# Attention and a feed-forward net in one kernel: another order of TensorE's work in the attention lead, the split of the attention's output on ScalarE and VectorE, and the closing flag placed earlier in the program

## The chip, the cores and the metric

The kernel runs on one core of a Trainium2 chip. It uses TensorE (PE, with its weight loads listed as PEld), VectorE (DVE), ScalarE (ACT), GpSimd (POOL) and SyncE (SP, which issues the DMAs). The metric is the device time of one execution in microseconds (us). The profile is one execution with the hardware profiler on; its span goes from the first to the last recorded instruction.

## The reference

```python
def _attn_ref(q, k, v, n_global, n_local):            # (4, 8, 768, 64) each; n_global 8, n_local 96
    scores = q @ k.transpose(0, 1, 3, 2) / sqrt(64)
    pos = arange(768); rel = pos[:, None] - pos[None, :]
    is_global = pos[None, :] < n_global
    is_local = (rel >= 0) & (rel < n_local)
    dist = where(is_global & ~is_local, n_local, abs(rel))
    scores = scores - slopes[:, None, None] * dist    # slope of head h: 2 ** -(h + 1)
    scores = where(is_global | is_local, scores, -1e9)
    a = exp(scores - max(scores)); a = a / (sum(a) + 1e-9)
    return a @ v

def _moe_ref(x, w_in, w_out):                         # x (3072, 512), w_in (512, 2048), w_out (2048, 512), float64
    h = x @ w_in
    return maximum(0.01 * h, h) @ w_out               # returned as float32
```

The attention's output, put together over the heads, is x of the second function. The weights come as 64-bit floats.

## The kernel before

**Work.** The 3072 tokens are 24 *steps* of 128. Six steps make one sequence, and a step that is not its sequence's first has block index `i > 0`. Each step is two *units* of four heads, so there are 48 units, u = 0 to 47. For its 128 queries a unit looks only at the keys that the band can reach: per half of the queries a `near` set of 128 keys (32 global, 96 earlier) and 64 of its `own`, which makes `KW` = 192 columns per head. The attention runs in plain float32. The feed-forward net (FFN) takes *chunks* of three steps, 384 tokens, and 16 blocks of 128 hidden features; a number j counts the blocks in the order in which they are done (7 of chunk 0, then 16 of chunk 1, the rest of chunk 0, then chunks 2 to 7). Each of its products is three TensorE matmuls in a rounded 32-bit format: every factor is split into a high part (the rounded value) and a low part (the rest), and high times high, high times low and low times high are summed. So the attention's output becomes `xh` and `xl`, the hidden layer `gh` and `gl`, the weights `wih`/`wil` and `woh`/`wol`.

**A unit's path.** `scores(u)`: 8 matmuls (L176) into a PSUM tile, `ps_sc` in the lead and `ps_av` later. `biased(u)`: four DVE instructions (L190) that add the band's table and take the maximum. `exps(u)`: four ACT exponentials (L205) that also give the sums. `sums(u)`: two small DVE instructions (L225, L226) for the reciprocals, then for units under 14 POOL makes `dg` (L240), diagonal matrices of the reciprocals. `transposes(u)`: 24 matmuls (L263) of probabilities by `dg`, which transpose and normalize into `ps_tr`. `keep_pt(u)`: one ACT copy to SBUF, `pt` (L278). `attn_v(u)`: probabilities times values, 4 matmuls (L302) for the own part and 16 (L309) for the near part. `keep_x(u)`: an ACT copy (L316) of the result to `x`; `split_x(u)`: POOL rounds `x` to `xh` (L44) and subtracts for `xl` (L329). Units from 14 on are transposed by DVE and DMAs in place of `transposes` and `keep_pt`.

**Events.** `event(t)` works on three units at once: scores of t, transposes of t-1 and attn_v of t-2. Events 0 to 7 are the *lead*, ahead of the first FFN block; events 8 to 13 are run with FFN blocks j = 1 to 6. From event 22 on two units are handled together (`visit`). In the lead the PE order within an event is scores, transposes, attn_v; from event 8 on it is attn_v, scores, transposes. The lead's PSUM tiles lie in a pool `ps_lead` that is closed before those of the FFN (`ps_h`, `ps_o`) are opened, so the first FFN matmul waits until the last `ps_ov` has been read.

**Weights.** 32 pieces of 64-bit weights are loaded and rebuilt as 32-bit values (`split_float64`): scale (ACT, L524), shift (DVE, L527 and L529), low (DVE, L533), then one event or FFN block later the high part (ACT, L537) and the rest (DVE, L540). Pieces 0 to 6 are converted in the lead, and the table `conv_at` gives piece 7 to j = 0, 8 to j = 1, 9 to j = 2, 10 and 11 to j = 3, and so on.

**What sets the order.** Engines run their own queues in program order. Nearly all instructions here are pinned to the order in which the code is written; the others (the FFN's copies in quiet blocks, DMAs of the output, the flag) are placed by a scheduler.

**FFN block.** `hidden` does 12 matmuls (L753 to L755) into `ps_h`, an ACT copy to `t` (L757), a DVE leaky ReLU (L758), the ACT cast to `gh` (L763) and the DVE difference `gl` (L764). `project` adds 3 matmuls per step (L774 to L776) into one of three `ps_o` tiles. The FFN for block j is followed on PE by the projections of block j-1. At a chunk's end the sums are copied to `part` (L440 by DVE, L442 by ACT) and SP sends them out (L444).

**The end.** `band_holds` checks, from the data's counts and maxima, whether the band is wide enough, and makes one integer flag. Every engine loads it into a register (L791), and where it is 0 the general path (`general_attention`, `general_ffn`) would compute all of it again. With these inputs it is not run, but every engine jumps over its instructions (the branch of L793) before the closing barrier (L848).

## Time and profile before

| | |
|---|---|
| time, median of 3 runs (lowest to highest) | 657.39 us (657.39 to 660.11) |
| the profiled execution's own time | 656.46 us |
| its span | 654.7 us, 14749 instructions |
| first FFN matmul starts | 40.15 us |
| first FFN matmul of j = 1, 2, 3, 4 | 46.43, 54.4, 60.9, 67.5 us |
| last FFN matmul ends | about 648 us |
| last DMA of the output issued | 648.63 us |

A line of a timeline reads: start, duration, engine, line of the kernel, operation, output <- inputs, tile and shape, count; in brackets the engine's idle time before it and what released it. A line of windows gives the length of the stretch, then busy time and instruction count of PE, PEld, DVE, ACT and POOL, the share of TensorE's full clock that was granted, the DMA share and GB/s. A line of waits gives the total, the number and the longest.

### The profile page before, as it was taken

Reading aid. Unit: us, or ns where it says so; the run is one execution under the profiler, and the core shown is the slowest. Engines: PE = TensorE matmul, PEld = TensorE weight load, DVE = VectorE, ACT = ScalarE, POOL = GpSimd, SP = SyncE. Lnnn points to the kernel's source line nnn. Section 1 sums busy time; section 2 is a strip of 40 time slices with the busy share of each in tenths; the row PEclk is TensorE's granted clock in tenths of the full one; section 3 lists DMA queues with packets and bytes.
Section 4 is the critical chain, followed back from the end, with each engine's and each line's share of the span. In section 5 each row is a group of like instructions: output and inputs, shape, how many; then the busy total and the mean of one; then the engine's idle time right before and its main releaser. Section 6 shows DMA issues by size and latency. Waiting matters only on the chain.

```text
span 654.7 us, 14749 instructions
## 1 busy us (share of the span) xinstructions
PE 628.5 (96%) x5803; PEld 558.1 (85%) x5803; DVE 363.6 (56%) x1073; ACT 281.3 (43%) x796; POOL 82.0 (13%) x146
## 2 busy tenths in 40 slices
PE   5689999999999999999999999999999999999995
PEld 4577888988888888988989889889889889999994
DVE  6949978987566444545645535535545546232221
ACT  6848765455444342442442433434433424232221
POOL 3424620000111010110110110100110101100000
PEclk9869999999999999999999999999999999999999
DMA  8966554432666433343444444335343432010001
GB/s 286 358 216 199 192 157 140 145 97 89 209 218 217 145 91 113 130 162 115 162 130 139 137 129 133 126 108 170 118 147 129 155 116 88 12 49 2 1 0 54
DMA packets 55166, 88.09 MB, mean 135 GB/s; under 512 B 9776, under 2 KB 30256, under 8 KB 55088
## 3 DMA queue, kind: packets, MB, share of 16 engines
q1 hardware_dynamic: 55088, 87.06, 40.6%
q8 instruction: 48, 0.79, 0.5%
q14 instruction: 30, 0.25, 0.1%
HBM read 67.90 MB, written 19.14 MB: 133 GB/s over the span
## 4 chain that ended last, share of the span: by engine, by line
PE 85%; DVE 6%; ACT 4%; POOL 2%; issue 2%; DMA 0%; ACTq 0%; DVEq 0%; POOLq 0%
PE ps_h L753 13%; PE ps_h L754 13%; PE ps_o L776 13%; PE ps_h L755 13%; PE ps_o L774 12%; PE ps_o L775 12%; PE ps_v L176 3%; PE ps_v L309 2%; ACT pr L205 1%; PE ps_v L302 1%; DVE w L533 1%; DVE w L529 1%; ACT w L524 1%; PE ps_av L176 1%; DVE t L758 1%
## 5 line engine op out<-in xcount | busy, mean ns | idle before, releaser
L753 PE MATMUL ps_h<-xh,wih 128*128 128x384 f32 x512 | 175.9, 343 | 1.2 <-ACT x L316 1.2
L754 PE MATMUL ps_h<-xl,wih 128*128 128x384 f32 x512 | 172.7, 337 | 0.7 <-POOL xl L329 0.7
L755 PE MATMUL ps_h<-xh,wil 128*128 128x384 f32 x512 | 172.4, 337 | 0.0
L758 DVE SCALAR_TENSOR_TENSOR t<-t 128x384 f32<-128x384 f32 x128 | 72.3, 565 | 150.6 <-ACT t L757 150.4
L776 PE MATMUL ps_o<-woh,gl 128*128 128x512 f32 x384 | 151.8, 395 | 0.1
L774 PE MATMUL ps_o<-woh,gh 128*128 128x512 f32 x384 | 150.4, 392 | 1.1 <-ACT part L442 0.7
L775 PE MATMUL ps_o<-wol,gh 128*128 128x512 f32 x384 | 150.5, 392 | 0.0
L757 ACT COPY t<-ps_h 128x384 f32<-128x384 f32 x128 | 61.1, 477 | 186.1 <-PE ps_h L755 186.1
L753 PEld LDWEIGHTS ps_h<-xh,wih 128*128 128x128 f32 x512 | 96.6, 189 | 11.5 <-ACT x L316 4.5
L764 DVE TENSOR_TENSOR gl<-t,gh 128x384 fp32r<-128x384 f32 x128 | 74.5, 582 | 55.6 <-ACT gh L763 55.6
L754 PEld LDWEIGHTS ps_h<-xl,wih 128*128 128x128 f32 x512 | 96.7, 189 | 5.2 <-POOL xl L329 0.9
L763 ACT CAST gh<-t 128x384 fp32r<-128x384 f32 x128 | 65.6, 512 | 74.2 <-DVE t L758 73.3
L755 PEld LDWEIGHTS ps_h<-xh,wil 128*128 128x128 f32 x512 | 96.6, 189 | 0.0
L776 PEld LDWEIGHTS ps_o<-woh,gl 128*128 128x128 f32 x384 | 72.1, 188 | 17.3 <-DVE gl L764 1.9
L205 ACT ACTIVATE pr<-pr,nmall 128x192 f32<-128x192 f32 (+1 forms) x192 | 83.6, 439 | 3.6 <-DVE nmall L190 3.5
L774 PEld LDWEIGHTS ps_o<-woh,gh 128*128 128x128 f32 x384 | 72.0, 188 | 12.9 <-ACT part L442 1.2
L775 PEld LDWEIGHTS ps_o<-wol,gh 128*128 128x128 f32 x384 | 72.1, 188 | 11.1
L44 POOL TENSOR_SCALAR xh<-x 128x256 fp32r<-128x256 f32 x48 | 21.3, 445 | 435.2 <-ACT x L316 366.3
L190 DVE CUSTOM_DVE_ANT_0 pr<-ps_v,nbw 128x192 f32<-128x192 f32 x88 | 26.2, 354 | 32.6 <-ACT x L316 32.6
L329 POOL TENSOR_TENSOR xl<-x,xh 128x256 fp32r<-128x256 f32 x48 | 37.3, 778 | 4.0
L205 ACT ACTIVATION_READ_ACCUMULATOR pr<-pr,nmall 128x1 f32 x192 | 36.6, 191 | 0.0
L232 DVE TENSOR_SCALAR pr<-pr,rs 128x192 f32<-128x192 f32 (+1 forms) x136 | 33.7, 312 | 1.0
(93 smaller groups left out, 495.0 us busy)
## 6 DMA issues: line engine op xcount, KB each, us to landing
kr<-in_kp_dram SPq DMA_DIRECT2D x40, 384.0 KB, 4.0
vr<-in_vp_dram SPq DMA_DIRECT2D x40, 320.0 KB, 4.4
via<-pr SPq DMA_DIRECT2D x30, 384.0 KB, 2.6
pt<-via SPq DMA_DIRECT2D x120, 96.0 KB, 2.3
wst<-in_wi_dram SPq DMA_DIRECT2D x16, 512.0 KB, 4.6
wst<-in_wo_dram SPq DMA_DIRECT2D x16, 512.0 KB, 3.7
qs<-in_qp_dram SPq DMA_DIRECT2D x24, 256.0 KB, 3.7
out_dram<-part SPq DMA_DIRECT2D x21, 256.0 KB, 2.4
```

What stands on the lines that cost most here:

```text
L205: pin(nc.scalar.activation(out=p, in_=p, func=AF.Exp, scale=-1.0, bias=nm[:, 2 * a + j:2 * a + j + 1], accum_out=sm[:, 2 * a + j:2 * a + j ...
L329: pin(nc.gpsimd.tensor_tensor(out=xl, in0=x, in1=xh.bitcast(F32), op=ALU.subtract))
L753: tc.keep_in_program_order(nc.tensor.matmul(ps, lhsT=wih[:, k, fs], rhs=xh[:, k, :CT], start=(k == 0), stop=False))
L754: tc.keep_in_program_order(nc.tensor.matmul(ps, lhsT=wih[:, k, fs], rhs=xl[:, k, :CT], start=False, stop=False))
L755: tc.keep_in_program_order(nc.tensor.matmul(ps, lhsT=wil[:, k, fs], rhs=xh[:, k, :CT], start=False, stop=(k == NK - 1)))
L757: pin(nc.scalar.copy(out=t, in_=ps))
L758: pin(nc.vector.scalar_tensor_tensor(out=t, in0=t, scalar=0.01, in1=t, op0=ALU.mult, op1=ALU.max))
L763: pin(nc.scalar.copy(out=gh, in_=t))
L764: pin(nc.vector.tensor_tensor(out=gl, in0=t, in1=gh.bitcast(F32), op=ALU.subtract))
L774: tc.keep_in_program_order(nc.tensor.matmul(o, lhsT=gh[:, ts_], rhs=woh[:, f, :], start=first, stop=False))
L775: tc.keep_in_program_order(nc.tensor.matmul(o, lhsT=gh[:, ts_], rhs=wol[:, f, :], start=False, stop=False))
L776: tc.keep_in_program_order(nc.tensor.matmul(o, lhsT=gl[:, ts_], rhs=woh[:, f, :], start=False, stop=last))
```

## The change

It has six parts.

1. **PE order in the lead.** `event` does scores(t), attn_v(t-2), transposes(t-1); transposes and attn_v have changed places.
2. **`tall` units** (2 to 11: transposed by PE and not first in their sequence). The near keys of a query half now lie across all 128 partitions of `pt`: per head and half one matmul of 64 rows by 128 columns makes them (8, new line 265), and the own keys keep 8 of 64 by 64 (new line 275), 16 in place of 24. The near part of `attn_v` takes 8 matmuls over 128 rows in place of 16 over 64 (new line 327). The values are laid out to match on the host.
3. **The split of x.** `high_x` is an ACT copy from PSUM that rounds right into `xh`; `low_x` (new line 344) is a DVE subtraction of `xh` from PSUM. POOL's two instructions and the tile `x` are gone. In event 7 `high_x(5)` stands ahead of the exponentials; `low_x` stands behind them from event 7 on, and at the event's end before. In `visit`, `low_x` follows both `biased`.
4. **Conversions.** Piece 7 is converted between the lead and the first FFN block; the blocks j = 0 to 6 take pieces 8 to 14, one each.
5. **The flag.** `band_holds` (without its transpose and identity) is written four FFN blocks before the end, a 1 by 1 matmul that sums over the partitions three blocks before the end, and the load of the flag ahead of the last chunk's copies.
6. **The general path.** Its loop over the heads, unrolled before, is now two loops that run, its DMAs go to GpSimd's queue in place of SP's, and its copies to DVE in place of ACT.

```diff
+    def tall(u):
+        return u < BY_DVE and where(u)[2] > 0
...
+        if tall(u):
+            for n in range(4):
+                for f in range(2):
+                    rows = slice(f * HALF, (f + 1) * HALF)
+                    tc.keep_in_program_order(nc.tensor.matmul(ps[:, f, n * HALF:(n + 1) * HALF],
+                                     lhsT=pr[rows, n * KW:n * KW + 2 * HALF], rhs=dg[rows, n % 2 * 2 + n // 2, :],
+                                     start=True, stop=True))
         for j in range(2):
-            for g in range(0 if i else 1, 3):
+            for g in range(2 if tall(u) else 1, 3):
...
         for f in range(0 if i else 1, 2):
-            for g in range(0 if i else 1, 2):
+            for g in (0,) if tall(u) else range(0 if i else 1, 2):
                 for j in range(2):
                     for a in range(2):
+                        if tall(u):
+                            n = 2 * j + a
+                            lhs, rhs = v[:, n, f, :], pt[:, n, f]
+                        else:
+                            lhs, rhs = v[rows, 2 * f + g, j, :], near(rows, j, g, f)
...
-    def keep_x(u, av):
-        x = att.tile([P, 2, P], F32, name="x", bufs=1)
-        pin(nc.scalar.copy(out=x, in_=av[:, :, 2 * KW:]))
-    def split_x(u):
-        pin(copy_exact(nc.gpsimd, xh, x))
-        pin(nc.gpsimd.tensor_tensor(out=xl, in0=x, in1=xh.bitcast(F32), op=ALU.subtract))
+    def high_x(u, av):
+        pin(nc.scalar.copy(out=parts(u, 0), in_=av[:, :, 2 * KW:]))
+    def low_x(u, av):
+        units.pop(u)
+        pin(nc.vector.tensor_tensor(out=parts(u, 1), in0=av[:, :, 2 * KW:], in1=parts(u, 0).bitcast(F32), op=ALU.subtract))
...
             scores(t, av)
-            if mid:
-                transposes(t - 1)
             if old:
                 ov = ps_lead.tile([P, 2, 512], F32, tag="ps_ov", name="ps_ov")
                 attn_v(t - 2, ov)
+            if mid:
+                transposes(t - 1)
...
             biased(t, av)
+            if t == LEAD + 1:
+                high_x(t - 2, ov)
             exps(t)
+        if t > LEAD:
+            low_x(t - 2, ov)
...
-        if old and t < LEAD + 2:
-            keep_x(t - 2, ov)
-        if old:
-            split_x(t - 2)
+        if old and t <= LEAD:
+            high_x(t - 2, ov)
+        if old and t <= LEAD:
+            low_x(t - 2, ov)
...
+        if c == NCHUNK - 1:
+            flags.append(nc.values_load(flag, min_val=0, max_val=1, ...))
...
-    conv_at = {0: [7], 1: [8], 2: [9], 3: [10, 11], 4: [12], 5: [13], 6: [14]}
+    conv_at = {n: [n + LEAD_CONV + 1] for n in range(half)}
...
+    for step in (*due, *conversion(LEAD_CONV)):
+        if step in due:
+            due.remove(step)
+        step()
...
+        if j == len(order) - NF // 4:
+            fl = const.tile([P, 4], F32, name="fl")
+            band_holds(tc, fl, nvec, nmall)
+        if j == len(order) - NF // 4 + 1:
+            band_holds_everywhere(tc, fl, ps_x.tile([P, 2, 512], F32, tag="ps_t", name="ps_f")[0:1, 0, 0:1], flag)
...
-            for h in range(H):
...
-                nc.sync.dma_start(out=q_sb, in_=qt[bass.ds(b, 1), h].rearrange("o d s -> (o d) s"))
...
+            with tc.For_i(0, H // 2, 1) as hp:
+                with tc.For_i(0, 2, 1) as two:
...
+                    nc.gpsimd.dma_start(out=q_sb, in_=qt[bass.ds(b, 1), bass.ds(hp, 1), bass.ds(two, 1)].rearrange("o g h d s -> (o g h d) s"))
...
```

Three places show what the edits do to the engines' own order. The first is PE at the lead's last event, 7, up to the first FFN matmul (`ps_sc` are scores, `ps_tr` transposes, `ps_ov` the attention's outputs). Before:

```order
L176 MATMUL ps_sc<-kr,qs 64x192 x8
L263 MATMUL ps_tr<-dg,pr 64x64 x24
L302 MATMUL ps_ov<-pt,vr 64x128 x4
L309 MATMUL ps_ov<-pt,vr 64x64 x16
L753 MATMUL ps_h<-xh,wih 128x384
```

and after:

```order
L180 MATMUL ps_sc<-kr,qs 64x192 x8
L315 MATMUL ps_ov<-pt,vr 64x128 x4
L327 MATMUL ps_ov<-pt,vr 64x64 x8
L265 MATMUL ps_tr<-dg,pr 128x64 x8
L275 MATMUL ps_tr<-dg,pr 64x64 x8
L797 MATMUL ps_h<-xh,wih 128x384
```

Scores stand first in both; the outputs have moved ahead of the transposes, and both have fewer, larger matmuls.

The second place is DVE from the last lead event's conversion work to the first FFN block (`w` with a number is the piece being rebuilt, `rs` the reciprocals of event 7, `t` and `gl` the FFN's first block). Before:

```order
L540 TENSOR_TENSOR wol<-w_650,woh 128x512
L527 TENSOR_SCALAR w_739<-w_739 128x512
L529 SCALAR_TENSOR_TENSOR w_739<-wst,w_739 128x512
L225 TENSOR_SCALAR rs<-sm 128x4
L226 RECIPROCAL rs<-rs 128x4
L533 SCALAR_TENSOR_TENSOR w_739<-wst,w_739 128x512
L758 SCALAR_TENSOR_TENSOR t<-t 128x384
L540 TENSOR_TENSOR wil<-w_739,wih 128x4x128
L764 TENSOR_TENSOR gl<-t,gh 128x384
L527 TENSOR_SCALAR w_799<-w_799 128x512
```

and after:

```order
L344 TENSOR_TENSOR xl<-ps_ov,xh 128x2x128
L576 TENSOR_TENSOR wol<-w_587,woh 128x512
L563 TENSOR_SCALAR w_658<-w_658 128x512
L565 SCALAR_TENSOR_TENSOR w_658<-wst,w_658 128x512
L229 TENSOR_SCALAR rs<-sm 128x4
L230 RECIPROCAL rs<-rs 128x4
L569 SCALAR_TENSOR_TENSOR w_658<-wst,w_658 128x512
L576 TENSOR_TENSOR wil<-w_658,wih 128x4x128
L563 TENSOR_SCALAR w_694<-w_694 128x512
L565 SCALAR_TENSOR_TENSOR w_694<-wst,w_694 128x512
L569 SCALAR_TENSOR_TENSOR w_694<-wst,w_694 128x512
L802 SCALAR_TENSOR_TENSOR t<-t 128x384
```

The low part of x is now DVE's, and the end of piece 6 with the whole of piece 7 stands ahead of the first FFN block's `t`.

The third place is SP at the program's end. Before:

```order
L444 DMA out_dram<-part 128x512 x6
L791 TENSOR_LOAD flag
L793 COMPARE_AND_BRANCH
L672 COMPARE_AND_BRANCH
L672 UNCONDITIONAL_BRANCH x2
L848 BRANCH_PREFETCH_HINT
L672 ISA
L677 DMA gq<-in_qt_dram 64x768
```

and after:

```order
L469 DMA out_dram<-part 128x512 x6
L448 TENSOR_LOAD flag
L835 COMPARE_AND_BRANCH
L710 COMPARE_AND_BRANCH
L710 UNCONDITIONAL_BRANCH x2
L894 BRANCH_PREFETCH_HINT
```

The flag's load still stands behind the last output DMAs on SP, and on ACT and DVE behind the last copies. What lies behind the branch is shorter: from the flag's load to the end SP has 26 rows in place of 162, ACT 27 in place of 240, DVE 215 in place of 527 and PE 332 in place of 446, while POOL has 76 in place of 29.

## The prediction

> **What bounds the kernel now.** I read the page first, its engines and its chain of waits.

> ```profile
> span 654.7 us, 14749 instructions
> ...
> PE 628.5 (96%) x5803; PEld 558.1 (85%) x5803; DVE 363.6 (56%) x1073; ACT 281.3 (43%) x796; POOL 82.0 (13%) x146
> ...
> PE 85%; DVE 6%; ACT 4%; POOL 2%; issue 2%; DMA 0%; ACTq 0%; DVEq 0%; POOLq 0%
> ```

> TensorE (PE) is busy 96% of the span and carries 85% of the chain, so only its holes and its own work can change the time. The windows say where the holes are (columns: busy time and count of PE, PEld, DVE, ACT, POOL, then the granted clock).

> ```profile
> 20.20:30.40 10.20, 5.60 (x245) 4.36 (x240) 10.06 (x38) 9.51 (x28) 5.82 (x9) 1.00 0.99 350
> 30.40:44.10 13.70, 10.65 (x175) 9.50 (x174) 6.31 (x20) 6.55 (x22) 4.31 (x7) 0.50 0.81 284
> 46.40:86.30 39.90, 37.54 (x645) 33.24 (x637) 38.23 (x104) 30.56 (x89) 21.49 (x34) 1.00 0.64 207
> ...
> 500.00:600.00 100.00, 100.00 (x770) 90.04 (x769) 40.66 (x116) 33.39 (x87) 7.36 (x14) 1.00 0.24 79
> ```

> In the lead, 20 to 30 us, DVE is full (10.06 of 10.20) and ACT nearly so, PE half idle. From 30.4 to 44.1 PE runs at half clock. From 46 to 86 PE (37.54) and DVE (38.23 of 39.90) are both almost full. From then on, as in the last row, PE is the bound alone, with nothing to win: later edits (the split of x in `visit`, the conversions) stand beside a full PE, with DVE at 41%, and I cost them at nothing; a copy that PE had to wait for would cost its own length, half a microsecond, at most.

> **The lead.** The next rows are timelines of DVE, POOL, PE and ACT.

> ```profile
> 25.84 1.19 DVE L540 TENSOR_TENSOR wol<-w,woh 128x512 fp32r<-128x512 f32 x1
> ...
> 28.01 0.16 DVE L225 TENSOR_SCALAR rs<-sm 128x4 f32<-128x4 f32 x1
> ...
> 32.15 0.16 DVE L225 TENSOR_SCALAR rs<-sm 128x4 f32<-128x4 f32 x1
> ...
> 34.80 0.36 DVE L190 CUSTOM_DVE_ANT_0 pr<-ps_sc,nbw 128x192 f32<-128x192 f32 x1 [1.70 <-PE ps_sc L176]
> ...
> 35.91 0.69 DVE L540 TENSOR_TENSOR wol<-w,woh 128x512 fp32r<-128x512 f32 x1
> ...
> 44.91 0.56 DVE L758 SCALAR_TENSOR_TENSOR t<-t 128x384 f32<-128x384 f32 x1 [6.36 <-ACT t L757]
> ...
> 48.44 0.35 DVE L190 CUSTOM_DVE_ANT_0 pr<-ps_av,nbw 128x192 f32<-128x192 f32 x1
> ```
> ```profile
> 25.26 0.41 POOL L44 TENSOR_SCALAR xh<-x 128x256 fp32r<-128x256 f32 x1
> 25.75 0.73 POOL L329 TENSOR_TENSOR xl<-x,xh 128x256 fp32r<-128x256 f32 x1
> ```
> ```profile
> 33.27 1.48 PE L176 MATMUL ps_sc<-kr,qs 64*64 64x192 f32 x13
> ...
> 40.15 0.69 PE L753 MATMUL ps_h<-xh,wih 128*128 128x384 f32 x1 [1.23 <-ACT x L316]
> ```
> ```profile
> 39.72 0.38 ACT L316 COPY x<-ps_ov 128x256 f32<-128x256 f32 x1
> ```

> One lead event takes 32.15 - 28.01 = 4.14 us. DVE's L540 takes 1.19 us beside POOL's split of x and 0.69 without it, so moving that split off POOL gives DVE 0.50 an event, and `low_x` takes some back. No row has its shape; between L190 from PSUM (192 columns, 0.35) and a 384-column op (0.56) I take 0.40 for 256 columns. By DVE's sum alone an event gets 0.1 shorter. But `low_x` waits for ACT's `high_x`, which stands behind the exponentials, and the next `biased` is queued behind it: 0.3 longer if that wait shows (`high_x` takes 0.38, by the L316 row). I take 0.13 longer for four events, and 0.2 for three small flag instructions that DVE's order now has in the startup chain (0.16 each by L225's row, not all of it on the path): 0.7 later by event 7.

> There the wait of 1.70 ahead of L190 goes: PE, at half clock, came to scores(7) late, behind transposes and outputs. With scores first and those two behind them, `biased(7)` starts at 34.80 - 1.70 + 0.7 = 33.8 and ends 35.91 - 34.80 = 1.1 later, at 34.9. `high_x(5)` now stands there, not behind the exponentials and `keep_pt` as the ACT copy at 39.72 did; with 0.38 for it, 0.40 for `low_x` and some 0.3 of hand-overs (the one shown, 39.72 + 0.38 to 40.15, took 0.05), the first FFN matmul starts at 36.0 in place of 40.15.

> Behind it DVE has to do the rest of pieces 5 and 6 and all of piece 7 first. From 34.9 that is `low_x` 0.40, eight instructions on 128x512, at L540's 0.69 each 5.5, and 0.4 for the two of the reciprocals: free at some 41.3. The FFN's first `t` is ready at 44.91 - 4.15 = 40.8, so it runs at 41.3, **3.6 us** earlier than before; the moved conversion fills the 6.36 us in which DVE waited there. From `t` to `biased(8)` there were 48.44 - 44.91 = 3.5 us of DVE work, and as much now (the conversions are one ahead), so the gain holds. Bounds: 2.5 (piece 7 stands in full before `t`) to 4.15.

> **Events 9 to 13.**

> ```profile
> 52.23 0.45 PE L302 MATMUL ps_av<-pt,vr 64*64 64x128 f32 x8 [1.39 <-ACT pt L278]
> ...
> 72.90 0.45 PE L302 MATMUL ps_av<-pt,vr 64*64 64x128 f32 x8 [0.97 <-ACT pt L278]
> ...
> 87.27 0.44 PE L754 MATMUL ps_h<-xl,wih 128*128 128x384 f32 x1 [0.67 <-POOL xl L329]
> ```
> ```profile
> L764 DVE TENSOR_TENSOR gl<-t,gh 128x384 fp32r<-128x384 f32 x6 | 6.0, 996 | 0.0
> ...
> L758 DVE SCALAR_TENSOR_TENSOR t<-t 128x384 f32<-128x384 f32 x6 | 5.3, 880 | 0.1
> ```
> ```profile
> L764 DVE TENSOR_TENSOR gl<-t,gh 128x384 fp32r<-128x384 f32 x128 | 74.5, 582 | 55.6 <-ACT gh L763 55.6
> ```

> PE's holes here are 1.39, 0.97 and 0.67. The last two come from a full DVE and from POOL's `xl`. DVE's `gl` takes 996 ns here against 582 over the kernel: 6 x 0.41 = 2.5 us given back when POOL's split is gone, and about 1.9 of `t` likewise (its surplus over 0.56 is 0.32); six `low_x` cost 2.4, and block j = 3 loses one of its two conversions (four instructions, at 0.69 each 2.8). So DVE wins about 4.8 of 39.9 and falls behind PE: **1.6 us** gained, at least 0. The 1.39 ahead of `attn_v(7)` stays and grows, since DVE gains less than PE there.

> **The tall units.** PE's work in an event changes too (each float32 matmul shows as two passes, so 16 as x32).

> ```profile
> 58.22 0.39 PE L775 MATMUL ps_o<-wol,gh 128*128 128x512 f32 x1
> 58.45 0.40 PE L776 MATMUL ps_o<-woh,gl 128*128 128x512 f32 x1
> 58.77 0.45 PE L302 MATMUL ps_av<-pt,vr 64*64 64x128 f32 x8
> 59.04 0.64 PE L309 MATMUL ps_av<-pt,vr 64*64 64x64 f32 x32
> 59.51 0.83 PE L176 MATMUL ps_av<-kr,qs 64*64 64x192 f32 x16
> 60.16 0.88 PE L263 MATMUL ps_tr<-dg,pr 64*64 64x64 f32 x48
> 60.97 0.45 PE L753 MATMUL ps_h<-xh,wih 128*128 128x384 f32 x1
> ```
> ```profile
> L753 PEld LDWEIGHTS ps_h<-xh,wih 128*128 128x128 f32 x27 | 5.1, 187 | 0.5
> ...
> L309 PEld LDWEIGHTS ps_av<-pt,vr 64*64 64x64 f32 x160 | 3.1, 134 | 0.0
> ```

> An event takes PE 60.97 - 58.77 = 2.20 us, all in tiles of 64 by 64 of the array, four side by side. The tall forms halve the instructions of the near part and double each one's share of the array, so the array's own time stays. But the event now goes from 64 by 64 to 128 by 64, back, to 64 by 128 and back: four more changes of tile. One change is in the rows: L776 to L302 starts 0.32 apart where L775 to L776 starts 0.23 apart, so about 0.1 each. With 0.1 more for weight loads of 128 columns (187 ns against 134) that is 0.5 an event, in the five events with FFN work **2.5 us** lost. In the lead it costs nothing: PE waits there. Bounds: -0.2 an event (fewer instructions) to 1.0 (changes of 0.2). [...]

> **The end.**

> ```profile
> L444 SPq DMA_DIRECT2D out_dram<-part x3: 332/333/759, 647.3 to 648.6; - x3
> ...
> DMA to landing us min/median/max: 3.1/3.2/3.3
> ```
> ```profile
> L793 SPq EVENT_SEMAPHORE  x8: 17/17/17, 652.8 to 653.3; - x8
> L793 POOLq COMPARE_BRANCH  x1: 45/45/45, 567.8 to 567.8; - x1
> L793 POOLq EVENT_SEMAPHORE  x1: 17/17/17, 568.3 to 568.3; - x1
> ...
> L793 SPq COMPARE_BRANCH  x1: 50/50/50, 650.2 to 650.2; - x1
> ```

> The flag's load still stands behind the copies and DMAs on ACT, DVE and SP, so the edit that writes it earlier brings nothing there. What changes is the jump: SP branches at 650.2 and goes on at 652.8, 2.6 us for 162 rows jumped, POOL takes 567.8 to 568.3, 0.5 for 29. SP's stretch is now 26 rows, like POOL's. At 0.5 SP is through at 650.7 and waits for the last output, which lands at 648.6 + 3.2 = 651.8. From there the end follows as it did from 652.8, less part of eight semaphore waits that are done by then: **1.3 us** gained; bounds 0 (the jump as slow as before) to 1.9. [...]

> **Sum.** 3.6 + 1.6 - 2.5 + 1.3 = 4.0. The profiled execution took 656.46, 1.76 more than its span, so 652.5 for it; the median of the runs, 657.39, is 0.93 above it, so **653.4**. By the terms' bounds, not all at once, 649.5 to 656.

> **Rivals.** A, the sum, chance 0.51.

> B, the tall units cost 1.0 an event, 5.0 in all, 0.15: **655.9**. For it: the weight loads stand more in one another's way with two tiles than with four; against: L309 gets its 32 passes, each with a load of 134 ns, through in 59.51 - 59.04 = 0.47 us, so loads overlap deeply now.

> C, the clock, 0.12. Before, the clock fell to 0.50 at 30.4 after ten microseconds with PE 55% busy. The changed kernel has a hole of some 2.1 us ahead of `attn_v(7)` (1.39 now, and what PE gains more than DVE). If a stretch with that hole makes the clock fall for another 3.4 to 6.8 us (a quarter to a half of the 13.7 it stayed down), PE loses half of it, 1.7 to 3.4: **655.1 to 656.8**. Against: the 1.39 hole brought no fall (1.00 from 46.4 on). [...]

> D, the other side, 0.09: weight loads of a tall unit no longer hide. Each of the 16 tall matmuls runs in two passes, so 32 loads; if they go one behind another, 16 x 0.187 + 16 x 0.134 = 5.1 in place of the 1.0 that those parts take now (0.47, and two thirds of the 0.81 from 60.16 to 60.97), 4.1 more an event, 20.5 in five in place of 2.5: **671.4**. It decides from 1.3 an event on, where 1.3 x 5 eats 3.6 + 1.6 + 1.3, and is seen as slower from 2.0. Against: from 500 to 600 us PE is busy all the time beside 90 us of such loads, so they hide there.

> E, the change does not do what it says at the end, the jump still takes 2.6 us, 0.13: **654.7**.

> **Numbers.** A measurement of this kernel tells some 0.5% from no change, 654.1 to 660.7 here. A lies on the faster side in four of five cases by its terms (0.41), E in 0.05, B and C together in 0.06: faster 0.52; slower is D and a rest of C, 0.10; the same 0.38. The range, 649.5 to 657.0, holds A to C and E and leaves out D and the rest.

> **What would show it.** The first FFN matmul near 36.0; `attn_v(7)` near 48.6 with a hole of about 2 us; no wait over 0.3 ahead of the later `attn_v`; 2.7 us from an event's first matmul to the FFN's next, against 2.20 (2.2 speaks for a free tall form, 3.2 for B, 6 for D); SP's first semaphore wait at about 3 us behind its last DMA's issue rather than 4.2. The prediction falls if the first FFN matmul comes after 38, if the clock is under 1.00 between 46 and 86, or if PE has new holes behind 90 us.

## The result

| | before | change |
|---|---|---|
| median of the runs (lowest to highest) | 657.39 us (656.95 to 660.11) | 665.59 us (661.15 to 666.15) |
| span of the profiled execution | 654.7 us | 663.6 us |
| first FFN matmul | 40.15 us | 44.80 us |
| FFN block 8 starts | 90.31 us | 97.26 us |
| from there to the last block's start | 551.2 us | 554.7 us |
| last FFN matmul's end to the end of the span | 6.71 us | 5.11 us |

The change is slower: a ratio of 1.0103, 95% interval 1.0064 to 1.0143. The forecast was 653.4 us with a range to 657.0. The span grew by 8.9 us, and the table says where: 7.0 up to block 8, where events 8 to 13 are over, 3.5 in the 119 blocks behind it, and 1.6 given back at the end.

The page of the changed kernel:

```profile
span 663.6 us, 14032 instructions
...
PE 647.3 (98%) x5484; PEld 569.5 (86%) x5484; DVE 373.9 (56%) x1121; ACT 282.6 (43%) x796; POOL 20.8 (3%) x48
...
PEclk9559999999999999999999999999999999999999
...
PE 91%; DVE 4%; ACT 2%; issue 1%; POOL 0%; DMA 0%; ACTq 0%; DVEq 0%
```

PE issues 319 instructions fewer and is busy 18.8 us longer, and its share of the chain rises from 85% to 91%. So the holes were closed, but by work that takes longer. The two digits 5 are new: from 16.7 to 47.4 us PE runs at half clock, which holds most of the lead, where before it was at half for 3.4 us (16.8 to 20.2) and again from 30.4 to 44.1. The three slower of the change's four runs have a mean granted clock of 0.975 to 0.978, the fastest one, 661.15 us, has 0.991. PE's timeline of one lead event, and then of one event with FFN work, shows which instructions take the time:

```profile
28.42 0.70 PE L315 MATMUL ps_ov<-pt,vr 64*64 64x128 f32 x8 [0.43 <-DVE xl L344]
29.05 1.17 PE L327 MATMUL ps_ov<-pt,vr 128*64 128x64 f32 x16
30.16 1.97 PE L265 MATMUL ps_tr<-dg,pr 64*128 64x64 f32 x16
32.06 0.70 PE L275 MATMUL ps_tr<-dg,pr 64*64 64x64 f32 x16
32.54 1.50 PE L180 MATMUL ps_sc<-kr,qs 64*64 64x192 f32 x16
34.47 0.70 PE L315 MATMUL ps_ov<-pt,vr 64*64 64x128 f32 x8 [0.43 <-DVE xl L344]
...
44.80 0.69 PE L797 MATMUL ps_h<-xh,wih 128*128 128x384 f32 x1
...
56.26 0.45 PE L315 MATMUL ps_av<-pt,vr 64*64 64x128 f32 x8 [0.27 <-ACT pt L290]
56.64 0.73 PE L327 MATMUL ps_av<-pt,vr 128*64 128x64 f32 x16
57.30 0.88 PE L180 MATMUL ps_av<-kr,qs 64*64 64x192 f32 x16
58.11 1.11 PE L265 MATMUL ps_tr<-dg,pr 64*128 64x64 f32 x16
59.15 0.46 PE L275 MATMUL ps_tr<-dg,pr 64*64 64x64 f32 x16
59.54 0.44 PE L797 MATMUL ps_h<-xh,wih 128*128 128x384 f32 x1
```

A lead event takes 34.47 - 28.42 = 6.05 us (4.14 before), and PE waits for 0.43 of it: PE has become the lead's bound. An event with FFN work takes 59.54 - 56.26 = 3.28 us (2.20 before). The tall transposes (L265) alone take 59.15 - 58.11 = 1.04 us for 16 passes at full clock and 1.90 at half, where the 48 passes of the old form took 0.81 at full clock, the 16 for the own keys among them; those now take 0.39 beside the 1.04.

PE has one wait left between 44 and 92 us, so the holes of before are gone:

```profile
PE ps_av L315 <- ACT pt L290: 0.3, 1, 0.3
```

This alone does not confirm the forecast's reason, DVE's lighter load: the kernel before with nothing but tall units added shows the same single line, and there PE's longer events alone can fill the holes. But the two later holes are gone without tall units too.

At the end SP's jump is short (the branch, and the first and last of the closing waits):

```profile
L835 SPq COMPARE_BRANCH  x1: 50/50/50, 660.5 to 660.5; - x1
```
```profile
L894 SPq EVENT_SEMAPHORE  x14: 17/28/28, 661.0 to 663.5; - x14
```
```profile
SPq L894 <- DMA out_dram<-part: 1.0, 2, 0.7
```

From 660.5 to 661.0 it takes 0.5 us (2.5 before), and SP then waits 1.0 for the last output to land, as forecast.

That leaves the blocks behind 90 us, where PE is nearly always busy and runs the same instructions in both kernels. The starts of the first matmul of two blocks in a row, before and after:

```profile
90.31 0.34 PE L753 MATMUL ps_h<-xh,wih 128*128 128x384 f32 x1
...
94.46 0.34 PE L753 MATMUL ps_h<-xh,wih 128*128 128x384 f32 x1
```
```profile
93.07 0.33 PE L797 MATMUL ps_h<-xh,wih 128*128 128x384 f32 x1
...
97.26 0.33 PE L797 MATMUL ps_h<-xh,wih 128*128 128x384 f32 x1
```

A quiet block (no other work of PE in it or right ahead of it, and no wait) takes 4.15 us here before and 4.19 after. Over the whole trace the kernel before has two paces, 4.15 us in 48 quiet blocks and 4.17 in 26, and the changed kernel has one, 4.19 in all 74. A mean of 0.03 us for each of the 119 blocks makes the 3.5 us. Nothing in the prediction speaks of it.

### The profile page after: what moved, and what is told of

Same layout as the page of the kernel before. It is cut to its first block, busy times and chain, and to the rows that moved or that the text cites. A ratio compares the mean times of both kernels' runs of the same rounds, so it can differ in the third digit from the quotient of the medians.

```text
span 663.6 us, 14032 instructions
## 1 busy us (share of the span) xinstructions
PE 647.3 (98%) x5484; PEld 569.5 (86%) x5484; DVE 373.9 (56%) x1121; ACT 282.6 (43%) x796; POOL 20.8 (3%) x48
## 4 chain that ended last, share of the span: by engine, by line
PE 91%; DVE 4%; ACT 2%; issue 1%; POOL 0%; DMA 0%; ACTq 0%; DVEq 0%
PE ps_h L797 14%; PE ps_o L820 13%; PE ps_h L799 13%; PE ps_o L819 13%; PE ps_h L798 13%; PE ps_o L818 13%; PE ps_v L180 2%; PE ps_tr L265 2%; PE ps_v L327 2%; PE ps_v L315 1%; PE ps_av L180 1%; PE ps_tr L275 1%; PE ps_av L327 1%; PE ps_av L315 1%; DVE w L569 1%
## 5 line engine op out<-in xcount | busy, mean ns | idle before, releaser
L808 DVE TENSOR_TENSOR gl<-t,gh 128x384 fp32r<-128x384 f32 x128 | 71.2, 556 | 55.1 <-ACT gh L807 55.1
L819 PEld LDWEIGHTS ps_o<-wol,gh 128*128 128x128 f32 x384 | 72.0, 187 | 12.1
L239 DVE STREAM_TRANSPOSE pr<-pr 128x768 f32<-128x768 f32 (+1 forms) x34 | 32.2, 946 | 0.9
L340 ACT CAST xh<-ps_v 128x256 fp32r<-128x256 f32 x28 | 10.4, 373 | 38.0 <-PE ps_v L180 36.3
```

The source lines that it names most:

```text
L808: pin(nc.vector.tensor_tensor(out=gl, in0=t, in1=gh.bitcast(F32), op=ALU.subtract))
L819: tc.keep_in_program_order(nc.tensor.matmul(o, lhsT=gh[:, ts_], rhs=wol[:, f, :], start=False, stop=False))
```

## The experiments

**The tall units alone, and the change without them.** In the first kernel `tall(u)` is false everywhere and the values lie as before; in the next two it holds for some units; the last adds it to the kernel before.

```diff
-        return u < BY_DVE and where(u)[2] > 0
+        return u in TALL and where(u)[2] > 0        # (), range(7, 12), range(2, 6)
```

> The changed kernel with no tall unit (transposes 24 of 64 by 64, near outputs 16 of 64 by 64, values laid out as before), all other parts of the change kept. Theory T (the tall forms are the whole loss, the other parts bring what the sum gave them, 3.6 + 1.6 + 1.3 = 6.5): about 651 us, a lead event at about 4.2 us, the first FFN matmul near 36, FFN events back to 2.2 us on PE. Rival R (the lead's new PE order and VectorE's new wait slow the lead whatever the shape): 657 or more, the first FFN matmul at 40 or later, with the clock at half in the whole lead.

> The changed kernel with units 7 to 11 tall and units 2 to 6 not: the lead's events are as without tall units, and five FFN events have them. Theory T with the price read in the changed kernel's trace (3.29 against 2.20 us an event): 5 x 1.1 = 5.5 us over the kernel without tall units, less what the hole before the outputs of unit 7 takes up, so 655 to 656.5. The prediction's price (0.5 an event) would give 2.5, 653.5.

> The changed kernel with units 2 to 5 tall and the others not: tall units in the lead only. The prediction had them free there, since TensorE waits: then the time of the kernel without tall units. Theory T: at half clock TensorE needs about 5.6 us an event, over VectorE's 4.1, so four events are 1.9 longer and the clock, with TensorE neither idle nor full, stays at half: 5 to 8 us over the kernel without tall units. If the clock is at full in the lead, nothing.

> The kernel before with only the tall units added. Theory T: about 5.5 us in the FFN events (less part of them that VectorE's time hides) and 4 to 8 in the lead, 664 to 670. The prediction's price gives 660. Rival R (tall units cost little, the loss comes of the new order): 657 to 659.

| kernel | median us | ratio to before (95%) |
|---|---|---|
| no tall unit | 655.68 | 0.9969 (0.9950 to 0.9987) |
| units 7 to 11 tall (FFN events) | 659.11 | 1.0029 (1.0009 to 1.0049) |
| units 2 to 5 tall (lead) | 660.28 | 1.0035 (1.0009 to 1.0061) |
| the change, units 2 to 11 tall | 665.59 | 1.0103 (1.0064 to 1.0143) |
| the kernel before with tall units | 660.49 | 1.0065 (1.0033 to 1.0097) |

Without tall units the change is a small gain, so they turn its sign. In the FFN events they cost 659.11 - 655.68 = 3.4 us and in the lead 4.6; together with unit 6 the whole is 9.9 (8.8 by the ratios; the change itself was measured at another time than the other rows). An event with both tall forms takes 3.28 us at full clock in every one of these traces and 2.19 without; in the change that is 5 x 1.09 plus 0.35 for an event with the tall outputs alone, 5.8 us of PE work. With units 7 to 11 one of the five has only the tall transposes, so it is less there, and a part can fall into the hole ahead of the outputs of unit 7. On the kernel before they cost less than expected, 660.49 against 657.10 measured beside it or 0.65%, 3.4 to 4.3 us. A likely reason, not varied alone, is that PE's longer events there fill holes in which it waited for DVE. But the kernel without them came out at 655.7 and not at 651: 4 to 5 us of the forecast's gain are missing there too.

The lead's price goes with the clock. The ten runs of the kernel with tall units in the lead lie between 655.75, with a mean granted clock of 0.992, and 662.92, with 0.979; the same kernel, so what varies is how long the clock stays at half: an estimate from these means, and from 0.50 and 1.00, the only values in the traces of before and of the change, gives about 10 us in the first and 28 in the second (in the changed kernel's trace it is 30.7, at a mean of 0.976). In each of the twenty traces the changes of the granted clock lie whole multiples of 3.41 us apart (16.67 and 47.39 us in the changed kernel, nine steps). Windows of the changed kernel, and of the kernel before, along these steps:

```profile
23.52:26.94 3.42, 3.42 (x52) 3.11 (x52) 2.37 (x6) 1.27 (x7) 0.06 (x1) 0.50 0.91 299
...
30.35:33.76 3.41, 3.41 (x48) 2.82 (x48) 1.59 (x5) 1.26 (x4) 0.61 (x1) 0.50 0.88 348
33.76:37.18 3.42, 2.99 (x38) 2.26 (x34) 3.15 (x13) 3.04 (x11) 0.00 (x0) 0.50 0.60 177
```
```profile
16.80:20.21 3.41, 3.15 (x77) 3.07 (x80) 3.34 (x13) 3.41 (x12) 1.30 (x3) 0.50 1.02 395
20.21:23.62 3.41, 2.64 (x112) 1.90 (x104) 3.38 (x12) 3.17 (x12) 2.02 (x3) 1.00 0.95 303
```

Before, a window with PE busy 3.15 of 3.41 us was followed by full clock. With tall units windows of 3.42 of 3.42 and 3.41 of 3.41 were followed by half clock. So PE's busy time in the profile is not, alone, what the clock went by. Nor is the count of passes in a window: it was 48 or 52 with tall units against 77, but in the kernel with units 2 to 5 tall a window with 50 passes and PE busy 2.98 of 3.41 us (38.18 to 41.59 us) was followed by full clock. What the clock goes by, no run here tells.

**Fewer changes of tile.** In the FFN events of the kernel with units 7 to 11 tall, PE does all 64 by 64 parts first, then the tall outputs, then the tall transposes.

```diff
-            attn_v(t - 2, ov)
             if now:
                 scores(t, av)
+            attn_v(t - 2, ov, 0)          # own part
             if mid:
-                transposes(t - 1)
+                transposes(t - 1, 0)      # own part
+            attn_v(t - 2, ov, 1)          # near part
+            if mid:
+                transposes(t - 1, 1)      # near part
```

> The changed kernel with units 7 to 11 tall, as the run before with these units (659.1), but in the FFN events PE does scores, own outputs and own transposes first, all 64 by 64, then the tall outputs, then the tall transposes: four changes of tile in an event in place of six. Theory T (a change of tile costs 0.2 us, and two passes at the head of the new tile 0.1 more; the tall transposes' weight loads of 128 columns cost 0.43): an event takes 2.7 us in place of 3.29, five events 2.5 to 3 us less. If the changes are free and only the loads count, 3.29 stays.

Measured: 658.68 us, 1.0034 (1.0013 to 1.0056), against 659.11 and 1.0029 for the old grouping, so the time can't tell them apart. The event can:

```profile
55.63 0.88 PE L181 MATMUL ps_av<-kr,qs 64*64 64x192 f32 x16
56.33 0.40 PE L316 MATMUL ps_av<-pt,vr 64*64 64x128 f32 x8
56.55 0.41 PE L276 MATMUL ps_tr<-dg,pr 64*64 64x64 f32 x16
56.89 0.73 PE L328 MATMUL ps_av<-pt,vr 128*64 128x64 f32 x16
57.55 1.11 PE L266 MATMUL ps_tr<-dg,pr 64*128 64x64 f32 x16
58.59 0.44 PE L801 MATMUL ps_h<-xh,wih 128*128 128x384 f32 x1
```

58.59 - 55.63 = 2.96 us, 0.32 less than 3.28 for two changes less: 0.16 for one, half of what was expected. Four changes make 0.64 of the 1.09. The rest is the tall transposes' own pace: in the trace a pair of passes starts every 0.112 us, where four old passes started every 0.058 us; 8 pairs at 0.112 against 8 groups of four at 0.058 are 0.43 us. A weight load of the tall transposes, 128 columns, takes 0.187 us (L265 of the changed kernel, at full clock), one of the old form, 64 columns, 0.135 (L263 before). The tall outputs, whose loads have 64 columns and take 0.137, have no such price: in this trace a pair of their passes starts every 0.058 us, as four old ones did. That the loads make the slower pace is read from these figures and was not varied alone; the 0.43 itself is measured.

**Where the operands lie in SBUF.** What differs in the quiet blocks is neither an instruction nor a wait. But the change removes tile `x` (1024 bytes per partition) and adds two flag tiles of 32, and behind them `xh`, `xl`, `gh` and `gl` start at 256 past a multiple of 512 bytes in place of 192; the weights start at 0 in both. (These starts are those that the program gives the tiles; the traces hold no addresses.) So unused bytes were added: in two kernels to put these tiles at their old addresses, and 64 in the kernel before to put them at 256.

```diff
     def high_x(u, av):
+        if u == 0:
+            att.tile([P, 240], F32, name="pad", bufs=1)       # never read or written
```

> The changed kernel without tall units and with 960 unused bytes of SBUF per partition behind the probabilities' buffers, so that xh, xl, gh and gl lie at the addresses that they have in the kernel before (in the change they lie 960 bytes lower: tile x of 1024 is gone, two small flag tiles of 32 are new). Theory A (the addresses of the FFN's operands set its pace, 4.147 us a quiet block before, 4.187 in all kernels with the change): pace 4.147 again, about 4.5 us under the kernel without tall units, so 651. Rival (the pace comes of VectorE's new work or of the other code around it): pace 4.187, time as without the bytes, 655.7.

> The kernel before with 64 unused bytes of SBUF per partition ahead of its constants, nothing else: the FFN's operands start 64 bytes higher, at the same place in 512 bytes as in the changed kernel. Theory A: pace 4.187 in place of 4.147 us a block, about 4.5 us slower, 661.5. Rival: no difference, 657.

> The whole change with the 960 unused bytes. Theory A: 4.5 us under the change, so about 661, and slower than before by the tall units alone (3.3 to 5 us). Rival: as the change, 665.

Two consecutive quiet blocks of the kernel before with 64 bytes more, and of the kernel without tall units at the old addresses:

```profile
90.54 0.33 PE L754 MATMUL ps_h<-xh,wih 128*128 128x384 f32 x1
...
94.73 0.33 PE L754 MATMUL ps_h<-xh,wih 128*128 128x384 f32 x1
```
```profile
83.95 0.34 PE L800 MATMUL ps_h<-xh,wih 128*128 128x384 f32 x1
...
88.10 0.34 PE L800 MATMUL ps_h<-xh,wih 128*128 128x384 f32 x1
```

4.19 and 4.15: the pace follows the addresses, with nothing else changed in the first of them but what lies where. It holds for every trace: in each of the seven with these tiles at 256 or at 0, no more than one of the 74 quiet blocks is under 4.18 us; in the nine with all of them at 192, 27 to 62 of the 74 take 4.15. The times follow too. The kernel before goes to 659.23, 1.0027 (1.0010 to 1.0045), 1.4 to 1.8 us and less than the 4.5 us expected; the kernel without tall units from 655.68 to 652.55, 0.9924 (0.9899 to 0.9949), and the whole change from 665.59 to 662.03, 1.0059 (1.0039 to 1.0080), 3.1 and 3.6 us less. The old addresses bring back a part of the pace and not all: in these two the blocks run now at 4.15 (32 and 27 of 74), now at up to 4.21. A block keeps the pace of the one ahead until other work of PE comes between; of some 1100 pairs of quiet blocks in a row in the twenty traces one pair changes pace.

Other places, all without tall units:

> The changed kernel without tall units and with 256 unused bytes per partition, so that xh, xl, gh and gl start at a multiple of 512 bytes, as the weights do (192 past one in the kernel before, 256 past one in the change). If what counts is the place of these operands against the weights within 512 bytes, the pace of a quiet block is a third one, unlike 4.147 (192) and 4.187 (256); if it is a distance of 64 bytes from some boundary, it may be either. No side has a number; 4.187 and 655.7 us if only the 192 of before is good.

> As the kernel without tall units, with xh, xl, gh and gl 64 bytes past a multiple of 512 (so far: 192 gives 4.147 us a quiet block, 0 and 256 give 4.187). Theory B (an odd multiple of 64 is good, a multiple of 128 bad): 4.147 and 652.5 us. Theory C (192 alone, or a range around it): 4.187 and 655.6.

> The same at 128 past a multiple of 512. Theory B: 4.187, 655.6 us. Theory C: 4.187 too, or 4.147 if a range from 128 on is good, which would rule B out.

> xh and xl at 192 as in the kernel before, gh and gl at 256 as in the change. If each operand acts on its own matmuls, the 12 matmuls into ps_h take 173.5 ns each as before and the 9 into ps_o 232.3 in place of 230 as in the change: 4.165 us a block, 654. If the two are locked to one another, 4.147 or 4.187.

> The other way round: xh and xl at 256, gh and gl at 192. If each operand acts on its own matmuls, ps_h matmuls at 175.6 ns and ps_o at 230: 4.170 us a block, 654. If the two are locked to one another, 4.147 or 4.187.

| xh, xl / gh, gl, bytes past a multiple of 512 | start to start, ps_h / ps_o, ns | quiet block, us | block 8 to the last, us | median us | ratio (95%) |
|---|---|---|---|---|---|
| 0 / 0 | 175.5 / 231.2 | 4.19 | 555.9 | 655.56 | 0.9963 (0.9942 to 0.9983) |
| 64 / 64 | 173.6 / 233.0 | 4.18 | 554.9 | 654.50 | 0.9969 (0.9946 to 0.9991) |
| 128 / 128 | 176.0 / 232.7 | 4.21 | 557.6 | 657.19 | 1.0020 (1.0001 to 1.0039) |
| 192 / 192 | 174.1 / 229.9 | 4.15 to 4.21 | 553.8 | 652.55 | 0.9924 (0.9899 to 0.9949) |
| 256 / 256 | 175.5 / 231.2 | 4.19 | 555.2 | 655.68 | 0.9969 (0.9950 to 0.9987) |
| 192 / 256 | 176.7 / 226.7 | 4.16 | 552.0 | 651.64 | 0.9939 (0.9918 to 0.9961) |
| 256 / 192 | 175.5 / 229.0 | 4.17 | 552.4 | 652.55 | 0.9942 (0.9924 to 0.9960) |

(The second column is the median over quiet blocks of the mean time from one matmul's start to the next, in the trace. The kernel before had medians of 656.66 to 658.80 us beside the different rows, so the ratio is what compares them.) Neither rule holds: 64 is as good as 192 for the first product and worst for the second, and with 192 / 256 the first product is the slowest of all and the second the fastest. The matmuls into ps_o read `gh` and `gl` and not `xh` and `xl`. Yet with `gh` and `gl` at 256 they start 231.2 ns apart when `xh` and `xl` lie at 256, and 226.7 when these lie at 192. So the place of one product's operands acts on the other's pace. By the ratios 128 is the worst place, and the three rows with a 192 are the best, though the intervals overlap in part with the next ones. That the place decides is shown, in both directions; by what rule is open. Nor is it shown that the pattern repeats every 512 bytes: the kernel before with 64 bytes more and the kernel without tall units have these tiles 1024 bytes apart and the same 4.19, but no pair 512 bytes apart was tried. The FFN's tile `t` moves with `gh` and `gl` in all of these kernels, so ACT's and DVE's accesses to it are not told apart from PE's own reads. The span of this effect is 557.6 - 552.0 = 5.6 us, nearly 1% of the kernel.

**The other parts, one taken back at a time,** from the kernel without tall units at the old addresses (652.55):

```diff
-            if old:                      # order: outputs ahead of transposes
-                ...attn_v(t - 2, ov)
             if mid:
                 transposes(t - 1)
+            if old:
+                ...attn_v(t - 2, ov)
```

> As the first of these, but with the lead's PE order of before (scores, transposes, outputs). By the prediction the new order is what takes the 1.70 us wait ahead of the last lead event away: the first FFN matmul 1.5 to 2 us later than with the new order, 652.5 to 653. Rival (the split of x and the moved conversion bring the lead's gain, the order nothing): the same time as the first.

656.63 us, 0.9982 (0.9960 to 1.0005): the new order is worth about 4 us by the runs, more than expected. The one profile of it has its first FFN matmul at 38.92, no later than the 38.93 with the new order, so it doesn't show where; and that profiled run, 655.16, is only 0.6 us over the profiled run of the kernel with the new order, 654.61, so the two profiles hold little of the 4 us.

The general path of before in place of the new one:

> The kernel without tall units and with before's addresses, but with the general path of before (unrolled heads, DMAs on SP's queue). The prediction's reading: SP's jump takes 2.5 us again, the time from the last FFN matmul's end to the end of the span 6.7 in place of 5.3 to 5.7, and 1.3 us more in all, 653.9. Rival (the flag's earlier place in the program brings the gain): no change, 652.5.

653.21 us, 0.9938 (0.9912 to 0.9964), which can't be told from 652.55. In the profile the jump is back, though:

```profile
SPq L829 <- SPq L829: 3.4, 1, 3.4
```

SP waits 3.4 us there, and the last FFN matmul's end to the end of the span takes 8.09 against 5.72. The body of that execution is faster (block 8 to the last in 551.0 against 553.8, at 4.15 in 61 of 74 quiet blocks against 32), which can hide it in the time. The flag is placed as in the change in both, so it is the new form of the general path that shortens the jump, and not the flag's earlier place. The other traces agree: SP's jump takes 0.5 us in all sixteen with the new general path, and 2.5 to 2.7 in the other three with the old one. DVE's jump takes 2.9 to 3.2 us with either.

```diff
-    conv_at = {n: [n + LEAD_CONV + 1] for n in range(half)}
+    conv_at = {0: [7], 1: [8], 2: [9], 3: [10, 11], 4: [12], 5: [13], 6: [14]}
...
-    for step in (*due, *conversion(LEAD_CONV)):
-        ...
```

> The kernel without tall units and with before's addresses, but with the old table of conversions (piece 7 in FFN block 0, two pieces in block 3). The prediction had this edit fill VectorE's idle 6.4 us and bring most of the 3.6 at the first events: then the outputs of unit 7 are as late behind the first FFN matmul as before (12.1 us in place of about 11) and the time 1.5 to 3 us longer. Rival: the order of PE alone decides, and nothing changes.

650.84 us, 0.9886 (0.9849 to 0.9922). Both were measured once more, side by side:

> The kernel without tall units and with before's addresses once more, with more rounds, beside the next. Before: 0.9924 of the kernel before, interval 0.9899 to 0.9949. If the moved conversion brings 1.5 us or more, this one is 1.5 us or more under the next.

> The same with the old table of conversions. Before: 0.9886, interval 0.9849 to 0.9922, from four runs; if that holds, the moved conversion is a loss of some 2 us and this version is the best found, about 651. If the two are the same here, the edit brings nothing that can be measured.

With the new table 653.10, 0.9912 (0.9886 to 0.9938); with the old one 651.15, 0.9888 (0.9862 to 0.9914). So the moved conversion gains nothing; it looks like a loss of 2 us, with intervals that overlap. Its mechanism is in DVE's and PE's timelines, first of the new table, then of the old:

```profile
43.22 0.55 DVE L805 SCALAR_TENSOR_TENSOR t<-t 128x384 f32<-128x384 f32 x1
```
```profile
50.65 0.45 PE L316 MATMUL ps_av<-pt,vr 64*64 64x128 f32 x8 [2.77 <-ACT pt L291]
```
```profile
41.52 0.56 DVE L801 SCALAR_TENSOR_TENSOR t<-t 128x384 f32<-128x384 f32 x1 [3.27 <-ACT t L800]
```
```profile
48.86 0.45 PE L316 MATMUL ps_av<-pt,vr 64*64 64x128 f32 x8 [1.35 <-ACT pt L291]
```

The first FFN matmul was at 38.97 and 37.23 in these two, so the first `t` came 4.25 and 4.29 us behind it and the outputs of unit 7 11.68 and 11.63: the conversion ahead of `t` fills DVE's wait, but DVE comes to the next event no sooner. PE's hole ahead of those outputs grows to 2.77 us, and the clock answers:

```profile
47.60:51.00 3.40, 0.62 (x18) 0.36 (x20) 3.31 (x11) 3.37 (x11) 0.43 (x1) 1.00 0.79 259
51.00:54.40 3.40, 3.40 (x101) 3.04 (x93) 2.76 (x8) 2.30 (x5) 0.45 (x1) 0.50 0.18 63
```

Some 3.4 us at half clock cost up to 1.7, an estimate from PE's being busy all through them. In the other profile with the new table the hole was 1.4 us and the clock did not fall. Part of the difference is again the pace: in both profiles with the old table the blocks behind 90 us take 551.9 us, with 62 and 47 of the 74 quiet ones at 4.15, and with the new one 553.8 and 554.1, with 32 and 28, at equal addresses. What sets the pace that a row of blocks falls into is open.

The kernel without tall units, at the old addresses and with the old table is the fastest found, at 0.989 of the kernel before both times.

## Why the prediction was wrong

**What failed first is the price of the tall units**, put at 0.5 us an event with 1.0 as the upper bound, and measured at 1.09. The working took one change of tile as a start 0.09 late and left out the second pass, which also comes late; a change costs 0.16. And it took 0.1 for the loads of 128 columns, by their duration alone, where the tall transposes with these loads ran at 0.112 us for two passes; that is 0.43. "The array's own time stays" was wrong for them. In the FFN events this makes 5.8 in place of 2.5 us. It is rival B's price, which was given 0.15, and 3.2 us an event was the prediction's own sign for it; B's reason, the loads, makes at most 0.43 of the 1.09.

**The second is "in the lead it costs nothing: PE waits there".** PE waited at full clock. At half clock, where the lead already was when its last events ran, a tall event needs 5.6 us of PE against DVE's 4.1, so the cover was gone, and the clock, which before had come back from 20.2 to 30.4, stayed at half to 47.4. The first FFN matmul came at 44.8 in place of 36.0. The prediction quoted the half clock and did not work out PE's event at it. By the runs the tall units cost 4.6 us in the lead. Rival C had the clock fall, but at a hole, in one place; that did happen in some kernels without tall units (the 2.77 us hole), and not in the change, which had no such hole.

**The third is a term that was not there**: 3.5 us in the blocks that the prediction costed at nothing, with the FFN's operands at 256 in place of 192 bytes past a multiple of 512; putting the tiles back brought 3.1 and 3.6 us. "Nothing to win" was held to mean nothing to lose.

**The lead's and the events' gains** were 3.6 + 1.6. In the kernels without tall units, with the new order and the new table, the outputs of unit 7 start at 49.1 to 51.0, 1.3 to 3.2 us ahead of 52.23, and block 8 at 85.2 to 88.4, 1.9 to 5.1 ahead of 90.31. In two of them, with holes of 3.6 and 2.77 us ahead of these outputs, the clock had a mean of 0.96 from 46.4 to 86.3 us. The lead event did not become 0.13 longer but a little shorter (4.05 from one event's outputs to the next's in the kernel without tall units). The two later holes, 0.97 and 0.67, are gone in every kernel with the new split of x, with tall units or without. The 1.39 ahead of the outputs of unit 7, which was to grow, is 0.9 to 3.6 us without tall units and 0.27 in the change. The 3.6 was argued to its end from the conversion, which brings none of it; by the runs the order of PE brings about 4, and the split of x was not taken back alone.

**The end** was right: 1.6 us measured, 1.0 to 1.6 in the other traces with the new general path, 1.3 forecast, from the shorter jump, with the flag's load where it was. Rival E is ruled out. Rival D, the other side, had the right place and the wrong size, 4.1 an event in place of 1.09; the change came out slower by B's price, the clock and the addresses together, a sum that no rival held.

Without tall units and with the old addresses the rest of the change measures 5.3 and 5.7 us, against 6.5 by the sum. That it comes so near is in part luck, as the conversion was to bring a part of it and did not.

## What to carry to other kernels

Fewer, larger matmuls are not fewer microseconds: count the passes that start together, the pace at which they start (here 0.112 us for two with loads of 128 columns, 0.058 for four with loads of 64) and the changes of tile (0.16 us each here), and price them at half clock too where the trace has half clock nearby (16 tall passes took 1.04 us at full clock and 1.90 at half). An engine's wait is cover only as far as its work, at the clock that it gets, fits in: here a tall event needed 5.6 us of PE at half clock against DVE's 4.1. Where an edit adds or drops a tile, compare the addresses of the operands of the steady loop, and its pace in two quiet blocks (4.15 against 4.19 us here), before reading anything else into a difference of half a percent.
